# Two attention blocks on one core: moving Q for the second one in two half runs per group, and transposing P in bf16

## The chip, the core and the metric

The kernel runs on one core of a Trainium2 chip. The core has a matrix engine (TensorE, in the profile PE, with its weight loads shown apart as PEld), a vector engine (VectorE, DVE), an activation engine (ScalarE, ACT), GpSimd (POOL) and SyncE (SP). Each engine works through its own queue in order; they meet only through semaphores. Matmuls read SBUF and write PSUM, which has eight banks of 2 KB per partition; DVE and ACT read PSUM and write SBUF. SP issues the transfers from HBM, which run on 16 DMA engines. The metric is the time of one execution on the device, in microseconds (us); lower is better.

## The reference

Two independent blocks of cached attention; their outputs are joined on the last axis.

```python
# both: B, Sq, D = 16, 32, 1024;  32 query heads, Dh = 128;  Sk = 1024;  bf16
# A: 4 key/value heads, each used by 8 query heads;  B: 32 key/value heads
q = (x @ wq).reshape(B, Sq, 32, Dh).transpose(0, 2, 1, 3)
scores = einsum("bhqd,bhkd->bhqk", q, k) * Dh ** -0.5
p = softmax(scores, axis=-1)
o = einsum("bhqk,bhkd->bhqd", p, v)
block = o.transpose(0, 2, 1, 3).reshape(B, Sq, 32 * Dh) @ wo
out = concatenate([block_A, block_B], axis=-1)
```

Block A's K and V caches are 16.8 MB each, block B's 134.2 MB each; with the weights nearly 340 MB go through the core once.

## The kernel before

**Quads.** The work of each attention is cut into 128 quads. A quad is 128 rows of scores (four times 32 query tokens) against 1,024 keys. For the first attention (A, `pi == 0`) a quad is one batch entry and four of the eight query heads that share one K/V head; for the second (B, `pi == 1`) it is two batch entries and two heads, so four K/V pairs. Four B quads form a group: 128 tokens (four batch entries) and four heads. One B step takes one B quad, usually one A quad, and a share of projections.

**Stages of a quad**, in `st_scores` to `st_oev`: scores in PSUM (two banks, `ps_s`); the row maximum on DVE (line 837); the exponential on ACT, which writes P in bf16 to SBUF and sums its rows (line 850); the transpose of P on PE (line 862) into one of the four general banks `ps_g`; its eviction to `PT_sb` by ACT or DVE (line 526); the product with V on PE (line 884 for A, 892 for B); normalisation (lines 908 and 909), transpose of the output (line 914) and its eviction. P is transposed as f32: two neighbouring bf16 values are taken as one f32 element, so 1,024 columns are 512 elements and four 128x128 transposes suffice, and every piece reads its 128 columns four f32 elements (16 bytes) apart. After it each transposed element holds a pair, and `ptc_of` takes every second bf16 value as the weights of the PV matmul. So that a pair belongs to neighbouring chunks in A too, A's exponential reads its scores with a jump of 128 elements (line 845).

**B's K** is transposed in 32x32 blocks by DVE, two words at a time (line 785), and A's K by PE in eight 128x128 bf16 transposes (line 776), one eviction each.

**B's Q.** `qprojB` projects the queries of one group and head block (line 616) and evicts them to `Qtok`, which has a place for each of two head blocks and four groups. `qprepB_tr` transposes one group's Q on DVE into `QBt` (line 625). `qprepB_sh` moves it across partitions: for each of the group's four batch entries `a`, four 32x32 matmuls with an identity (line 638) copy row group `a` of `QBt` to all four row groups of one PSUM bank, 256 columns wide, and an eviction of 128x256 writes `QR`, the scores' weights. In step t of a group only `a = t % 4` of the next group is moved (line 1066).

**Order of the work.** The program adds operations to a list with their dependencies, and `list_schedule` simulates the engines with the durations in `DUR` and orders every engine's queue by it. Operations marked `any` go to ACT or DVE, whichever the simulation finds better. General banks, P, PT and other buffers are given out during that simulation (`slot_time`, `acquire`); banks of kind `pj` (projections and Q's move) have two of the four in reserve. The order in the queues is fixed from then on, and `finalize` adds semaphore waits. Between two operations of PE no wait is added (`_needs_wait`). All transfers are issued from SP's queue: B's V (line 763) waits for the PV that frees one of three buffers, B's K (line 750) for the DVE transpose that frees one of four.

Of the kernel before, what the change touches and what calls it, by code (L numbers as in the profile page):

```python
# [15 lines left out]
SCHED = True  # L16
NVB_SLOTS = 3
NKB_SLOTS = 2
LAZY_PER_STEP = 100
# [6 lines left out]
PRIO_BONUS = {}  # L26
PE_MODE = {"scoresB": 2, "Qshuf": 2, "PVB": 1}
MODE_SWITCH = 0.05
# [6 lines left out]
DUR = {  # L35
    "scoresB": (0.216, 0.20), "scoresA": (0.216, 0.20), "PT_trA": (0.49, 0.22), "PT_trB": (0.49, 0.22), "PVA": (0.45, 0.22), "PVB": (0.112, 0.22),
    "OT_tr": (0.056, 0.22), "KTA_tr": (0.45, 0.22), "Qshuf": (0.107, 0.20), "qprojA": (0.432, 0.20), "qprojB": (0.432, 0.20),
    "oprojA": (0.432, 0.20), "oprojB": (0.432, 0.20), "xT_tr": (0.45, 0.22),
    "exp": (1.10, 0.12), "PT_ev@act": (0.466, 0.13), "norm@act": (0.25, 0.13), "OT_ev@act": (0.11, 0.13), "KTA_ev@act": (0.466, 0.13),
    "qA_ev@act": (0.47, 0.13), "qB_ev@act": (0.478, 0.13), "QR_ev@act": (0.252, 0.13), "acc0@act": (0.47, 0.13), "acc0@dve": (0.58, 0.12), "xT_ev@act": (0.90, 0.13),  # L40
    "o_fin@act": (0.47, 0.13),
    "KBt_tr": (1.126, 0.11), "max": (1.12, 0.11), "recip": (0.06, 0.11), "norm@dve": (0.23, 0.13), "PT_ev@dve": (0.58, 0.12),
    "OT_ev@dve": (0.08, 0.12), "KTA_ev@dve": (0.58, 0.12), "QBt_tr": (0.345, 0.10), "acc+": (0.58, 0.12), "accF": (0.59, 0.12),
    "qA_ev@dve": (0.58, 0.12), "qB_ev@dve": (0.58, 0.12), "xT_ev@dve": (0.60, 0.12), "o_fin@dve": (0.58, 0.12), "QR_ev@dve": (0.30, 0.12),
    "c0": (0.2, 0.1), "c1": (0.3, 0.1),
# [60 lines left out]
class Prog:  # L106
# [116 lines left out]
    def list_schedule(self, lat=0.05, look=LOOK):  # L223
# [43 lines left out]
        def slot_time(i):  # L267

            t = 0.0
            for v in acq[i]:  # L270
# [40 lines left out]
        while True:  # L311
# [119 lines left out]
def build(nc, pa, pb, out):  # L431
# [34 lines left out]
    with stack:  # L466
# [6 lines left out]
        ident = sb("ident", [P, P], BF)  # L473
        zeros = sb("zeros", [P, P], BF)
        id32 = sb("id32", [P, P], F32)
        z32 = sb("z32", [P, P], F32)
# [34 lines left out]
        pr.add("pool", lambda g: g.memset(zeros[:], 0.0), writes=["zeros"], name="c0")  # L511
        pr.add("pool", lambda g: g.affine_select(ident[:], zeros[:], [[1, P]], ALU.not_equal, 1.0, base=0, channel_multiplier=-1),
               reads=["zeros"], writes=["ident"], name="c1")
        pr.add("pool", lambda g: g.memset(z32[:], 0.0), writes=["z32"], name="c0")
        pr.add("pool", lambda g: g.affine_select(id32[:], z32[:], [[1, P]], ALU.not_equal, 1.0, base=0, channel_multiplier=-1),
               reads=["z32"], writes=["id32"], name="c1")

# [89 lines left out]
        def qprojB(m_, G):  # L607
            lazy_flush(("wq", 1, m_))

            JS = 2 if DJ % 2 == 0 else 1  # L610
            v = Virt("bank", "pj")
            for j0 in range(0, DJ, JS):
                def e_qp(e, j0=j0):
                    last = None
                    for j in range(j0, j0 + JS):
                        last = e.matmul(bank(v)[:, 0:CW], xT_sb[:, 1, j, G * P:(G + 1) * P], wq_sb[:, 1, j, :], start=(j == 0), stop=(j == DJ - 1))  # L616
                    return last
                pcs = sorted(set(j * WQP // DJ for j in range(j0, j0 + JS)))
                pr.add("pe", e_qp, reads=[("wq", 1, k_) for k_ in pcs] + [("xT", 1, G)], writes=[v], claims=[("Qtok", m_ % 2, G)], name="qprojB", dur=0.225 * JS,
                       rtag=dict((("wq", 1, k_), m_) for k_ in pcs))  # L620
            evac(Qtok[:, m_ % 2, G, :], lambda: bank(v)[:, 0:CW], reads=[], writes=[v, ("Qtok", m_ % 2, G)], name="qB_ev",
                 wtag={("Qtok", m_ % 2, G): m_}, mul=scale)

        def qprepB_tr(m_, G):
            pr.add("dve", lambda e: e.transpose(QBt[:, :].bitcast(F32), Qtok[:, m_ % 2, G, :].bitcast(F32)),
                   reads=[("Qtok", m_ % 2, G)], writes=["QBt"], name="QBt_tr", rtag={("Qtok", m_ % 2, G): m_}, wtag={"QBt": (m_, G)})

        def qprepB_sh(m_, G, a_list):
            gp = (m_ * NG + G) % 2
            for a in a_list:  # L630
                v = Virt("bank", "pj")

                def e_sh(e, a=a, v=v):
                    last = None
                    for rg in range(4):
                        e_ = rg // 2
                        rhs = QBt[32 * a:32 * a + 32, :].rearrange("p (hp e x) -> p e hp x", hp=2, e=2)[:, e_, :, :]
                        last = e.matmul(bank(v)[32 * rg:32 * rg + 32, 0:2 * Dh].rearrange("p (hp x) -> p hp x", hp=2),
                                        ident[32 * a:32 * a + 32, 32 * a:32 * a + 32], rhs, start=True, stop=True,
                                        tile_position=(32 * a, 32 * rg))  # L640
                    return last
                pr.add("pe", e_sh, reads=["QBt", "ident"], writes=[v], claims=[("QR", gp, a)], name="Qshuf", rtag={"QBt": (m_, G)})
                evac(QR[:, gp, a, :, :], lambda v=v: bank(v)[:, 0:2 * Dh].rearrange("p (hp x) -> p hp x", hp=2), reads=[],
                     writes=[v, ("QR", gp, a)], name="QR_ev", wtag={("QR", gp, a): (m_, G)})

# [194 lines left out]
        def st_exp(q):  # L840
            vS, vP, vst = q.vS, q.vP, q.vst

            def emit(e):
                if q.pi == 0:
                    src = ps_s[:, vS.idx, :, :].rearrange("p u n -> p (u n)").rearrange("p (c k) -> p k c", c=NCH)
                    dst = P_sb[:, vP.idx, :].rearrange("p (k c) -> p k c", c=NCH)
                else:
                    src = ps_s[:, vS.idx, :, :].rearrange("p g (s j) -> p g j s", s=16)
                    dst = P_sb[:, vP.idx, :].rearrange("p (g j s) -> p g j s", g=2, s=16)
                return e.activation(dst, src, ACTF.Exp, bias=stat[:, vst.idx, 0:1], scale=1.0, accum_out=stat[:, vst.idx, 1:2])  # L850
            pr.add("act", emit, writes=vS.res + [vP, vst], name="exp")

        NPK = NCH // 2

        def st_ptr(q):
            vP, vPT, vb = q.vP, q.vPT, q.vbt

            def e_pt(e):
                last = None
                p32 = P_sb[:, vP.idx, :].bitcast(F32)  # L860
                for m in range(NPK):
                    last = e.transpose(bank(vb)[:, m * P:(m + 1) * P], p32[:, m:Sk // 2:NPK], id32[:])  # L862
                return last
            pr.add("pe", e_pt, reads=[vP, "id32", vPT], writes=[vb], name="PT_trA" if q.pi == 0 else "PT_trB")

# [145 lines left out]
        qprepB_tr(0, 0)  # L1011
        qprepB_sh(0, 0, [0, 1, 2, 3])
        for hh in range(MS):
# [37 lines left out]
        for t in range(NIT):  # L1051
# [73 lines left out]
```

## Time and profile before

| what | value |
|---|---|
| median of three runs | 903.89 us (901.42, 905.68, 903.89) |
| span of the profiled execution, first to last instruction | 902.6 us |
| mean granted TensorE clock | 0.985 |
| moved by DMA | 341.67 MB, mean 379 GB/s |
| transposes of P (line 862) on PE | 177.0 us busy, 1,024 pieces |
| exponentials (line 850) on ACT | 285.8 us busy, 256 |
| Q's move for B (line 638) on PE | 41.0 us busy, 512 matmuls |

The profiled execution's time is known as its span; the median of the runs shown is 1.3 us longer. "Busy" is the share of the span in which an engine had an instruction under way; on PE a matmul's time includes the pipeline, which the next one overlaps, so PE's cost is better read from the distance between starts. A group's line gives the line of the kernel, the engine, the operation, output and input tiles, the shape, the number, busy time, mean ns of one, and the idle time of the engine just before these instructions with what ended it.

### The profile page before, as it was taken

How to read it: one execution, taken by the hardware profiler on the slowest of the kernel's cores; microseconds unless marked ns; L12 is line 12 of the kernel's file. 1: busy time of each engine (PE TensorE's matmuls, PEld its weight loads, DVE VectorE, ACT ScalarE, POOL GpSimd, SP SyncE). 2: the span in 40 equal slices, each digit the busy share in tenths (PEclk: the TensorE clock that was granted, in tenths of full speed). 3: DMA queues.
4: the chain of work that ended last, by engine and by line, in shares of the span. 5: the costliest groups of instructions: out<-in, count | busy, mean ns of one | idle time of the engine just before them, and what ended most of it. 6: DMA issues, size and time to landing. Idle time of an engine off the chain costs nothing.

```text
span 902.6 us, 29455 instructions
## 1 busy us (share of the span) xinstructions
PE 836.3 (93%) x12864; PEld 481.8 (53%) x12864; DVE 745.3 (83%) x1057; ACT 610.8 (68%) x1384; POOL 1.1 (0%) x8
## 2 busy tenths in 40 slices
PE   6999999999899999999999998999998988999886
PEld 4365555555555555555545455555555554555453
DVE  0578897888887999689887899878979788798885
ACT  3477886677666776676776466776867666586763
POOL 0000000000000000000000000000000000000000
PEclk9999999999999999999999999999999999999999
DMA  9999999999999999999999999999999999999994
GB/s 325 383 389 393 386 385 392 390 393 383 392 387 389 393 380 388 380 386 376 387 385 391 394 369 389 388 393 370 388 387 391 392 391 367 344 393 393 393 377 170
DMA packets 153984, 341.67 MB, mean 379 GB/s; under 512 B 12544, under 2 KB 28928, under 8 KB 153856
## 3 DMA queue, kind: packets, MB, share of 16 engines
q1 hardware_dynamic: 153856, 339.79, 100.6%
q8 instruction: 102, 1.67, 0.8%
q14 instruction: 26, 0.21, 0.1%
HBM read 337.64 MB, written 2.10 MB: 376 GB/s over the span
## 4 chain that ended last, share of the span: by engine, by line
PE 48%; DMA 23%; DVE 19%; ACT 8%; SPq 1%; issue 1%; ACTq 0%; DVEq 0%
DMA KB_sb<-in_B_k_cache_dram 21%; PE ps_s L827 10%; PE ps_g L862 9%; DVE stat L837 8%; DVE KBt_sb L785 8%; PE ps_g L680 6%; ACT P_sb L850 5%; PE ps_g L892 4%; PE ps_g L598 4%; PE ps_g L884 4%; PE ps_g L616 3%; PE ps_s L806 3%; PE ps_g L776 2%; ACT PT_sb L526 1%; PE ps_g L914 1%
## 5 line engine op out<-in xcount | busy, mean ns | idle before, releaser
L785 DVE STREAM_TRANSPOSE KBt_sb<-KB_sb 128x1024 f32<-128x1024 f32 x256 | 311.8, 1231 | 42.5 <-DMA KB_sb<-in_B_k_cache_dram 40.4
L837 DVE TENSOR_REDUCE stat<-ps_s 128x1 f32<-128x1024 f32 x256 | 304.7, 1209 | 50.7 <-PE ps_s L827 34.3
L850 ACT ACTIVATE P_sb<-ps_s,stat 128x1024 bf16<-128x1024 f32 x256 | 285.8, 1119 | 51.5 <-DVE stat L837 50.0
L862 PE MATMUL ps_g<-id,P_sb 128*128 128x128 f32 x1024 | 177.0, 300 | 13.0 <-ACT P_sb L850 4.7
L862 PEld LDWEIGHTS ps_g<-id,P_sb 128*128 128x128 f32 x1024 | 150.5, 207 | 54.9 <-issue 11.1
L827 PE MATMUL ps_s<-KBt_sb,QR 32*32 32x512 bf16 x4096 | 157.2, 399 | 19.5 <-ACT P_sb L850 10.9
L526 ACT COPY PT_sb<-ps_g 128x512 f32<-128x512 f32 x234 | 134.9, 591 | 59.5 <-PE ps_g L862 58.3
L908 ACT ACTIVATE O_sb<-ps_g,stat 128x128 bf16<-128x128 f32 x199 | 71.4, 370 | 63.0 <-PE ps_g L892 32.4
L806 PE MATMUL ps_s<-KTA_sb,QT_sb 128*128 128x512 bf16 x256 | 91.5, 388 | 6.0 <-ACT P_sb L850 5.6
L827 PEld LDWEIGHTS ps_s<-KBt_sb,QR 32*32 32x32 bf16 x4096 | 49.3, 90 | 81.1 <-ACT P_sb L850 17.8
L892 PE MATMUL ps_g<-VB_sb,PT_sb 128*32 128x128 bf16 x4096 | 91.1, 224 | 1.4 <-ACT PT_sb L526 0.9
L892 PEld LDWEIGHTS ps_g<-VB_sb,PT_sb 128*32 128x32 bf16 x4096 | 60.2, 97 | 48.7 <-issue 29.2
L884 PE MATMUL ps_g<-VA_sb,PT_sb 128*128 128x128 bf16 x1024 | 78.8, 220 | 1.8 <-ACT PT_sb L526 0.7
L884 PEld LDWEIGHTS ps_g<-VA_sb,PT_sb 128*128 128x128 bf16 x1024 | 61.6, 98 | 28.2 <-issue 8.5
L616 PE MATMUL ps_g<-wq_sb,xT_sb 128*128 128x512 bf16 x256 | 71.4, 386 | 2.9 <-DMA wq_sb<-in_B_wq_dram 2.8
L680 PE MATMUL ps_g<-woB_sb,OTB_sb 128*128 128x512 bf16 x256 | 68.7, 381 | 4.4 <-ACT OTB_sb L526 1.8
L598 PE MATMUL ps_g<-xT_sb,wq_sb 128*128 128x512 bf16 x256 | 72.0, 385 | 0.3
L680 PE MATMUL ps_g<-woA_sb,OTA_sb 128*128 128x512 bf16 x256 | 63.0, 380 | 1.3 <-DVE OTA_sb L526 1.0
L914 PE MATMUL ps_g<-ident,O_sb 128*128 128x128 bf16 x256 | 51.8, 224 | 3.0 <-ACT O_sb L908 2.0
L850 ACT ACTIVATION_READ_ACCUMULATOR P_sb<-ps_s,stat 128x1 f32 x256 | 51.8, 202 | 0.0
L526 ACT COPY OTA_sb<-ps_g 128x64 f32<-128x64 f32 x114 | 24.7, 216 | 36.7 <-PE ps_g L914 36.1
L691 DVE TENSOR_TENSOR acc<-acc,ps_g 128x512 f32<-128x512 f32 x64 | 41.2, 675 | 8.1 <-PE ps_g L680 7.6
(41 smaller groups left out, 537.5 us busy)
## 6 DMA issues: line engine op xcount, KB each, us to landing
VB_sb<-in_B_v_cache_dram SPq DMA_DIRECT2D x256, 512.0 KB, 8.1
KB_sb<-in_B_k_cache_dram SPq DMA_DIRECT2D x256, 512.0 KB, 9.2
KA_sb<-in_A_k_cache_dram SPq DMA_DIRECT2D x64, 256.0 KB, 7.7
VA_sb<-in_A_v_cache_dram SPq DMA_DIRECT2D x64, 256.0 KB, 8.1
wq_sb<-in_B_wq_dram SPq DMA_DIRECT2D x32, 256.0 KB, 8.6
wq_sb<-in_A_wq_dram SPq DMA_DIRECT2D x32, 256.0 KB, 8.8
woB_sb<-in_B_wo_dram SPq DMA_DIRECT2D x32, 256.0 KB, 9.2
woA_sb<-in_A_wo_dram SPq DMA_DIRECT2D x32, 256.0 KB, 9.1
```

The costliest lines, as they stand in the source:

```text
L526: return e.copy(dst, src) if hasattr(e, "activation") else e.tensor_copy(dst, src)
L598: last = e.matmul(bank(v)[:, 0:tn], wq_sb[:, 0, j, hc * Dh:(hc + 1) * Dh], xT_sb[:, 0, j, t0:t0 + tn], start=(j == 0), stop=(j == DJ - 1))
L616: last = e.matmul(bank(v)[:, 0:CW], xT_sb[:, 1, j, G * P:(G + 1) * P], wq_sb[:, 1, j, :], start=(j == 0), stop=(j == DJ - 1))
L680: last = e.matmul(bank(v)[:, 0:OUTW], OT[:, gp, hh, :], wo_[:, hh, oh * OUTW:(oh + 1) * OUTW], start=(hh == 0), stop=(hh == nh - 1))
L785: pr.add("dve", lambda e: e.transpose(KBt_sb[:, sl, t_, :].bitcast(F32), KB_sb[:, rs, :].bitcast(F32)), reads=[("KB", rs)], writes=[("KBt" ...
L806: pr.add("pe", lambda e, u=u: e.matmul(ps_s[:, vS.idx, u, :], qt[:, q.b, q.hh0:q.hh0 + 4, :].rearrange("p a q -> p (a q)"), KTA_sb[:, sl, ...
L827: last = e.matmul(ps_s[32 * cg:32 * cg + 32, vS.idx, g2, :].rearrange("p (s j) -> p s j", s=16), lhsT, rhs, start=(fp == 0), stop=(fp == 3 ...
L837: pr.add("dve", lambda e: e.tensor_reduce(stat[:, vst.idx, 0:1], ps_s[:, vS.idx, :, :], AXIS.XY, ALU.max, negate=True), writes=vS.res + [v ...
L850: return e.activation(dst, src, ACTF.Exp, bias=stat[:, vst.idx, 0:1], scale=1.0, accum_out=stat[:, vst.idx, 1:2])
L862: last = e.transpose(bank(vb)[:, m * P:(m + 1) * P], p32[:, m:Sk // 2:NPK], id32[:])
L884: last = e.matmul(bank(vb)[:, 0:Dh], ptc_of(vPT, c, 0, P), VA_sb[:, kvs, c, :], start=(c == 0), stop=(c == NCH - 1))
L892: last = e.matmul(bank(vb)[32 * a:32 * a + 32, 0:Dh], ptc_of(vPT, c, 32 * a, 32 * a + 32), VB_sb[:, kvs, a // 2, a % 2, c, :], start=(c == ...
```

## The change

1. P is transposed as bf16: eight 128x128 pieces into the same bank, `P_sb[:, c*128:(c+1)*128]` for A and `P_sb[:, c:1024:8]` for B. The eviction stays one 128x512 f32 copy. A's exponential reads its scores in order; PV takes its weights without gaps. The f32 identity goes, and the bf16 one is made in place.
2. All of a group's Q is moved in one step (`t % 4 == 0`), in two half runs: `Qshuf` for entries 0 and 2, `Qshuf2` for 1 and 3, eight matmuls each. Entries 0 and 1 fill one bank, 2 and 3 the other, and each bank is evicted by one 128x512 operation. Both half runs write both banks, so `Qshuf2` waits for `Qshuf`: the first wait of PE for itself. The planner's bank test now counts two banks taken by one operation.
3. `Qtok` is a ring of five group slots instead of eight.
4. Planned durations: transposes of P 0.49 -> 0.45, Q's moves 0.107 -> 0.15, their evictions 0.252 -> 0.478 (ACT) and 0.30 -> 0.58 (DVE).

```diff
+        if (d.name, op.name) == ("Qshuf", "Qshuf2"):
+            return True
...
-                if len(idle) <= keep:
+                if len(idle) <= keep + nth:
                     return None
-                t = max(t, sorted(idle)[0])
+                t = max(t, sorted(idle)[nth])
...
-                same_pe = (op.dma_key is None and beng == uo.eng and uo.eng == "pe")
+                same_pe = (op.dma_key is None and beng == uo.eng and uo.eng == "pe" and uo.name != "Qshuf2")
...
-        Qtok = sb("Qtok", [P, 2, NG, CW], BF)
+        Qtok = sb("Qtok", [P, NQT, CW], BF)
...
+            vv = [Virt("bank", "pj"), Virt("bank", "pj")]
+
+            def e_sh(e, aa):
+                last = None
+                for a in aa:
+                    out_ = bank(vv[a // 2])[:, (a % 2) * 2 * Dh:(a % 2 + 1) * 2 * Dh].rearrange("p (hp x) -> p hp x", hp=2)
+                    src_ = QBt[32 * a:32 * a + 32, :].rearrange("p (hp e x) -> p e hp x", hp=2, e=2)
                     for rg in range(4):
...
+                        last = e.matmul(out_[32 * rg:32 * rg + 32], ident[32 * a:32 * a + 32, 32 * a:32 * a + 32], src_[:, rg // 2, :, :],
+                                        start=True, stop=True, tile_position=(32 * a, 32 * rg))
+                return last
+            for name, aa in (("Qshuf", (0, 2)), ("Qshuf2", (1, 3))):
+                pr.add("pe", lambda e, aa=aa: e_sh(e, aa), reads=["QBt", "ident"], writes=vv, claims=[("QR", gp, a) for a in aa], name=name,
+                       rtag={"QBt": (m_, G)})
+            for b in range(2):
+                evac(QR[:, gp, 2 * b:2 * b + 2, :, :].rearrange("p a hp x -> p (a hp x)"), lambda b=b: bank(vv[b]), reads=[],
+                     writes=[vv[b], ("QR", gp, 2 * b), ("QR", gp, 2 * b + 1)], name="QR_ev",
...
-                    src = ps_s[:, vS.idx, :, :].rearrange("p u n -> p (u n)").rearrange("p (c k) -> p k c", c=NCH)
-                    dst = P_sb[:, vP.idx, :].rearrange("p (k c) -> p k c", c=NCH)
+                    src = ps_s[:, vS.idx, :, :].rearrange("p u n -> p (u n)")
+                    dst = P_sb[:, vP.idx, :]
...
-                p32 = P_sb[:, vP.idx, :].bitcast(F32)
-                for m in range(NPK):
-                    last = e.transpose(bank(vb)[:, m * P:(m + 1) * P], p32[:, m:Sk // 2:NPK], id32[:])
+                for c in range(NCH):
+                    pc = P_sb[:, vP.idx, c * P:(c + 1) * P] if q.pi == 0 else P_sb[:, vP.idx, c:Sk:NCH]
+                    last = e.transpose(bankb(vb)[:, c * P:(c + 1) * P], pc, ident[:])
...
-            return PT_sb[:, vPT.idx, :, :].rearrange("p c q -> p (c q)").rearrange("p (m r two) -> p m r two", m=NPK, two=2)[:, c // 2, lo:hi, c % 2]
+            return PT_sb[:, vPT.idx, c, lo:hi]
...
                 if t % 4 == 0:
                     qprepB_tr(qn.m, qn.G)
-                qprepB_sh(qn.m, qn.G, [t % 4])
+                    qprepB_sh(qn.m, qn.G)
```

More of the change, by code (lines that the diff above doesn't have):

```diff
@@ L17 @@
 NVB_SLOTS = 3
+NQT = 5
 NKB_SLOTS = 2
@@ L26 @@
 PRIO_BONUS = {}
-PE_MODE = {"scoresB": 2, "Qshuf": 2, "PVB": 1}
+PE_MODE = {"scoresB": 2, "Qshuf": 2, "Qshuf2": 2, "PVB": 1}
 MODE_SWITCH = 0.05
@@ L43 @@
     "OT_ev@dve": (0.08, 0.12), "KTA_ev@dve": (0.58, 0.12), "QBt_tr": (0.345, 0.10), "acc+": (0.58, 0.12), "accF": (0.59, 0.12),
-    "qA_ev@dve": (0.58, 0.12), "qB_ev@dve": (0.58, 0.12), "xT_ev@dve": (0.60, 0.12), "o_fin@dve": (0.58, 0.12), "QR_ev@dve": (0.30, 0.12),
+    "qA_ev@dve": (0.58, 0.12), "qB_ev@dve": (0.58, 0.12), "xT_ev@dve": (0.60, 0.12), "o_fin@dve": (0.58, 0.12), "QR_ev@dve": (0.58, 0.12),
     "c0": (0.2, 0.1), "c1": (0.3, 0.1),
@@ L269, in slot_time @@
             t = 0.0
-            for v in acq[i]:
+            for k_, v in enumerate(acq[i]):
+                nth = sum(1 for w in acq[i][:k_] if w.cls == v.cls)
                 idle = [slot_free[v.cls][x] for x in range(SLOTS[v.cls]) if held[v.cls][x] is None]
                 keep = sum(k for kind, k in BANK_RESERVE.items() if kind != v.kind and not any(h is not None and h.kind == kind for h in held["bank"])) if v.cls == "bank" else 0
-                if len(idle) <= keep:
+                if len(idle) <= keep + nth:
                     return None
-                t = max(t, sorted(idle)[0])
+                t = max(t, sorted(idle)[nth])
             return t
@@ L509, in build @@
             print("sbuf bytes remaining per partition:", nc.sbuf_bytes_remaining() if callable(nc.sbuf_bytes_remaining) else nc.sbuf_bytes_remaining)
[L511 to L516, printed above, removed]
+        pr.add("pool", lambda g: g.memset(ident[:], 0.0), writes=["ident"], name="c0")
+        pr.add("pool", lambda g: g.affine_select(ident[:], ident[:], [[1, P]], ALU.not_equal, 1.0, base=0, channel_multiplier=-1),
+               writes=["ident"], name="c1")
         def evac(dst_ap, src_ap, reads, writes, name, eng=None, wtag=None, rtag=None, mul=None):
@@ L618, in qprojB @@
                 pcs = sorted(set(j * WQP // DJ for j in range(j0, j0 + JS)))
-                pr.add("pe", e_qp, reads=[("wq", 1, k_) for k_ in pcs] + [("xT", 1, G)], writes=[v], claims=[("Qtok", m_ % 2, G)], name="qprojB", dur=0.225 * JS,
+                pr.add("pe", e_qp, reads=[("wq", 1, k_) for k_ in pcs] + [("xT", 1, G)], writes=[v], claims=[("Qtok", (m_ * NG + G) % NQT)], name="qprojB", dur=0.225 * JS,
                        rtag=dict((("wq", 1, k_), m_) for k_ in pcs))
-            evac(Qtok[:, m_ % 2, G, :], lambda: bank(v)[:, 0:CW], reads=[], writes=[v, ("Qtok", m_ % 2, G)], name="qB_ev",
-                 wtag={("Qtok", m_ % 2, G): m_}, mul=scale)
+            qs = (m_ * NG + G) % NQT
@@ L624, in qprepB_tr @@
+            evac(Qtok[:, qs, :], lambda: bank(v)[:, 0:CW], reads=[], writes=[v, ("Qtok", qs)], name="qB_ev",
+                 wtag={("Qtok", qs): (m_, G)}, mul=scale)
         def qprepB_tr(m_, G):
-            pr.add("dve", lambda e: e.transpose(QBt[:, :].bitcast(F32), Qtok[:, m_ % 2, G, :].bitcast(F32)),
-                   reads=[("Qtok", m_ % 2, G)], writes=["QBt"], name="QBt_tr", rtag={("Qtok", m_ % 2, G): m_}, wtag={"QBt": (m_, G)})
-        def qprepB_sh(m_, G, a_list):
+            qs = (m_ * NG + G) % NQT
@@ L629, in qprepB_sh @@
+            pr.add("dve", lambda e: e.transpose(QBt[:, :].bitcast(F32), Qtok[:, qs, :].bitcast(F32)),
+                   reads=[("Qtok", qs)], writes=["QBt"], name="QBt_tr", rtag={("Qtok", qs): (m_, G)}, wtag={"QBt": (m_, G)})
+        def qprepB_sh(m_, G):
             gp = (m_ * NG + G) % 2
[L630 to L634, printed above, removed]
-                    for rg in range(4):
[L636 to L644, printed above, removed]
@@ new lines, in qprepB_sh @@
+            for name, aa in (("Qshuf", (0, 2)), ("Qshuf2", (1, 3))):
[4 more added lines that the diff above has]
+                     writes=[vv[b], ("QR", gp, 2 * b), ("QR", gp, 2 * b + 1)], name="QR_ev",
+                     wtag={("QR", gp, 2 * b): (m_, G), ("QR", gp, 2 * b + 1): (m_, G)})
@@ L851, in st_exp @@
             pr.add("act", emit, writes=vS.res + [vP, vst], name="exp")
-        NPK = NCH // 2
         def st_ptr(q):
@@ L859, in e_pt @@
                 last = None
-                p32 = P_sb[:, vP.idx, :].bitcast(F32)
-                for m in range(NPK):
-                    last = e.transpose(bank(vb)[:, m * P:(m + 1) * P], p32[:, m:Sk // 2:NPK], id32[:])
+                for c in range(NCH):
+                    pc = P_sb[:, vP.idx, c * P:(c + 1) * P] if q.pi == 0 else P_sb[:, vP.idx, c:Sk:NCH]
+                    last = e.transpose(bankb(vb)[:, c * P:(c + 1) * P], pc, ident[:])
                 return last
-            pr.add("pe", e_pt, reads=[vP, "id32", vPT], writes=[vb], name="PT_trA" if q.pi == 0 else "PT_trB")
+            pr.add("pe", e_pt, reads=[vP, "ident", vPT], writes=[vb], name="PT_trA" if q.pi == 0 else "PT_trB")
         def st_pev(q, eng=None):
@@ L1011, in build @@
         qprepB_tr(0, 0)
-        qprepB_sh(0, 0, [0, 1, 2, 3])
+        qprepB_sh(0, 0)
         for hh in range(MS):
```

9 lines of the change are left out of this document (3 added, 6 removed).

## The prediction

> **What bounds the kernel now.** First the profile's page: engine totals, the bandwidth row, and the chain that ended last.
>
> ```profile
> PE 836.3 (93%) x12864; PEld 481.8 (53%) x12864; DVE 745.3 (83%) x1057; ACT 610.8 (68%) x1384; POOL 1.1 (0%) x8
> GB/s 325 383 389 393 386 385 392 390 393 383 392 387 389 393 380 388 380 386 376 387 385 391 394 369 389 388 393 370 388 387 391 392 391 367 344 393 393 393 377 170
> q1 hardware_dynamic: 153856, 339.79, 100.6%
> PE 48%; DMA 23%; DVE 19%; ACT 8%; SPq 1%; issue 1%; ACTq 0%; DVEq 0%
> ```
>
> The bandwidth row has a ceiling of 393 GB/s that many slices reach and none but one (394) passes. A slice is 902.6 / 40 = 22.56 us. Summing (393 - rate) / 393 x 22.56 us gives 3.9 us lost in the first slice, 12.8 us in the last and only 16.5 us in all 38 between. So the transfers are nearly the bound: if compute never held them up again in the middle, the span would be 902.6 - 16.5 = 886 us. No saving on an engine can bring more than that, short of the two ends. PE's 93% says that there is little room the other way.
>
> Next the groups by shape, for the operations that the change touches and for their nearest neighbours.
>
> ```profile
> L850 ACT ACTIVATE P_sb<-ps_s,stat 128x1024 bf16<-128x1024 f32 x256 | 285.8, 1119 | 51.5 <-DVE stat L837 50.0
> L862 PE MATMUL ps_g<-id,P_sb 128*128 128x128 f32 x1024 | 177.0, 300 | 13.0 <-ACT P_sb L850 4.7 <-ACT OTA_sb L526 3.2 <-ACT OTB_sb L526 1.8
> L776 PE MATMUL ps_g<-ident,KA_sb 128*128 128x128 bf16 x512 | 39.2, 219 | 1.1 <-ACT OTA_sb L526 0.7 <-DVE acc L691 0.4
> L638 PE MATMUL ps_g<-QBt,ident 32*32 32x256 bf16 x512 | 41.0, 277 | 2.0 <-DVE acc L691 1.0 <-ACT acc L526 0.7
> L526 ACT CAST QR<-ps_g 128x256 bf16<-128x256 f32 x101 | 37.8, 381 | 14.7 <-PE ps_g L638 11.8 <-PE ps_s L827 1.9
> L526 DVE CAST QR<-ps_g 128x256 bf16<-128x256 f32 x27 | 11.0, 411 | 0.9 <-PE ps_g L638 0.8
> L526 ACT COPY KTA_sb<-ps_g 128x512 f32<-128x512 f32 x46 | 27.5, 597 | 5.2 <-PE ps_g L776 5.1
> L526 ACT COPY xT_sb<-ps_g 128x1024 bf16<-128x1024 bf16 x6 | 5.8, 1015 | 4.7 <-PE ps_g L546 4.7
> ```
>
> A matmul's duration includes pipeline time that the next one overlaps, so its cost is read from starts on PE's timeline:
>
> ```profile
> 304.57 0.28 PE L638 MATMUL ps_g<-QBt,ident 32*32 32x256 bf16 x2
> 305.16 0.29 PE L638 MATMUL ps_g<-QBt,ident 32*32 32x256 bf16 x4
> 305.38 0.75 PE L862 MATMUL ps_g<-id,P_sb 128*128 128x128 f32 x4
> 305.97 0.59 PE L616 MATMUL ps_g<-wq_sb,xT_sb 128*128 128x512 bf16 x2
> 306.40 0.61 PE L776 MATMUL ps_g<-ident,KA_sb 128*128 128x128 bf16 x8
> 306.85 0.59 PE L616 MATMUL ps_g<-wq_sb,xT_sb 128*128 128x512 bf16 x2
> ```
>
> Four f32 transposes hold PE 305.97 - 305.38 = 0.59 us; eight bf16 ones (of KA_sb, stored without gaps) 306.85 - 306.40 = 0.45 us, although there are twice as many. Over the whole timeline the medians are 0.58 and 0.54 us, since the run of eight is often followed by a 32-row operation, and then its last piece takes 0.149 us in place of 0.056: changing between tilings costs about 0.09 us.
>
> Last, who holds the transfers up, on SP's queue:
>
> ```profile
> SPq L763 <- PE ps_g L892: 136.7, 69, 7.4
> SPq L750 <- DVE KBt_sb L785: 115.2, 77, 5.2
> ```
>
> SP waits for a PV to free a V buffer, or for the DVE to free a K buffer. Issues take 8 to 9 us to land at 393 GB/s, so most of this waiting passes while earlier transfers still flow.
>
> **The change, part by part.**
>
> P's transposes. 1,024 f32 pieces go, 2,048 bf16 pieces come. For the first attention the pieces are now gapless, like KA_sb's: 0.58 -> 0.54 us per quad. For the second they step by 8 bf16, 16 bytes, and no bf16 weight load in the trace does that. Bounds: the row of KA_sb (0.056 us a piece), and the f32 pieces, which step by the same 16 bytes: (0.75 - 0.29) / 3 = 0.15 us at most, about 0.12 in the longer runs. I take the KA_sb value, because element type and shape agree with it, and PT_sb's reads at line 884, with a step of 4 bytes, also run at 0.056. Then PE's demand falls by 256 x 0.04 = 10 us. Line 862 holds 8.7% of the chain, 78.5 us, so 78.5 x 0.04 / 0.58 = 5.4 us leave the path.
>
> [...]
>
> Exponential of the first attention. Its PSUM read is now without gaps (it jumped 128 f32 per element). Both forms take 1.12 us now, and both jump. Bounds: no change, and the gapless 1,024-element copy at 1.015 us, -0.10 us. That row is a copy from bf16, so I take the middle, -0.05: 128 x 0.05 = 6 us of ACT. L850 is 4.9% of the chain, 44 us, half of it the first attention's: 22 x 0.05 / 1.12 = 1 us of path.
>
> Q's move. 128 runs of four matmuls become 64 of eight; all 512 matmuls stay. Entering the 32-row tiling 64 times fewer saves up to 64 x 0.09 = 5.8 us on PE; at PE's 48% of the chain, 2.8 us of path. Evictions: 37.8 + 11.0 = 48.8 us on ACT and DVE become 64 x 0.597 = 38.2 us, -10 us. L526 for QR is not among the chain's listed lines, so I count nothing; that cover is lost only where scores wait for QR.
>
> The added wait. The second half run waits for the first to finish. Lower bound 0 (other PE work is placed between; the planner now makes it ready 0.40 us after the first starts); upper bound a whole matmul, 0.28 us, and about 0.1 us of signalling. I take 0.15: 32 x 0.15 = 4.8 us of PE, 2.3 of path. Behind it stand all later PE operations, so ACT's PT and O evictions and SP's V loads inherit what is not filled.
>
> Two banks at once. Of four general banks a group holds two until both are evicted; before, one four times. The bank time is less (two evictions of 0.6 for four of 0.38 with their own waits), the peak is higher. From 0 to 0.4 us of delay per group to the PT and PV that find no bank; I take 0 and keep the rest for a rival.
>
> Nothing: the Qtok ring. Group g's slot was last read by group g-5's DVE transpose, planned at second-attention step 4(g-6), which is at least five steps (some 35 us) before the projection that refills it. Also nothing: two POOL operations fewer at 0.7 to 2.0 us, since PE's first use waits for x until 3.52 us; contiguous weights for PV, at 0.056 already. No DMA is moved by name; the planner reorders SP's issues by new durations, of either sign, perhaps 3 us.
>
> Sum on the path: -5.4 - 1 - 2.8 + 2.3 = -6.9 us, well inside the 16.5. The profiled execution's span 902.6 becomes 895.7; the median of the runs shown, 903.9, is 1.3 above that span, so **897 us**.
>
> **Rivals.**
>
> *Hidden (no change, 904 us).* The dips come from DVE, not PE: K transposes and maxima are 312 + 305 us of DVE and alternate on the chain. For: 115 us of SP's waits end on L785. Against: the larger 137 end on PV. Then the 6.9 us only lengthen waits.
>
> *Strided pieces slow (928 us, slower).* If each 16-byte step costs a piece of the second attention 0.12 us, as the f32 pieces with this step do, a run becomes 8 x 0.12 + 0.09 = 1.05 us: +0.47 x 128 = 60 us, less 5 for the first attention and about 6 elsewhere, +49 us on PE. PE has 902.6 - 836.3 = 66 us idle; half absorbed gives 902.6 + 24.5 + 1.3 = 928, all absorbed 904, none 953. It decides once a piece exceeds 0.58 / 8 = 0.073 us. For: the only row with this step is slow. Against: that row is f32 as well, and cannot separate the two.
>
> [...]
>
> *Bank squeeze (911 us, slower).* Two banks taken together stall PT and PV by 0.4 us in each of 32 groups, 13 us, against savings of half the 6.9. For: evictions of 0.6 us hold both; PE already waits for bank-freeing ACT lines. Against: a bank is busy under half the time by the sums of the rows.
>
> **How the numbers follow.** Forecast 0.44 (own range 891 to 902: dips recovered twice as much, or almost not), hidden 0.18, strided 0.22, squeeze 0.16. Half a per cent, 4.5 us, is what a measurement tells (the runs span 901.4 to 905.7). Faster: 0.33 of the forecast's and 0.02 of the hidden = 0.35. Same: 0.11 + 0.14 + 0.02 of the squeeze = 0.27. Slower: 0.22 + 0.14 + 0.02 = 0.38. Range 890 to 926: it leaves out the upper half of the strided case (0.11) and 0.03 below.
>
> **What would show it.** L862's successor: bf16 starts 0.056 us apart in the first attention (right); in the second 0.056 (forecast) or 0.1 and above (strided rival), with PE busy up by some 50 us. L850: a first-attention form below the second's 1.12. QR evictions: 64 of about 0.6. PE idle ended by PE itself at the second half run: under 5 us. Middle bandwidth losses down from 16.5 to about 10 us. PT waiting for bank-freeing evictions, up by 10 us, would speak for the squeeze; unchanged dips with more idle PE for the hidden case.

## The result

The changed kernel takes 898.5 us (897.8 to 900.9, four runs) against 904.75 us for the kernel before on the same chip: a ratio of 0.994, 95% interval 0.9915 to 0.9966, faster by 0.6%. These two times are medians, 6.3 us apart; the means, 898.9 and 904.1 us, whose quotient is the ratio, are 5.2 us apart. The forecast was 897 us. Its direction and its size came out; the runs below show that its reason did not.

The profiled execution's span fell from 902.6 to 896.0 us. The granted clock was 0.985 in the first and 0.998 in the second of these executions; a second profile of the changed kernel, at 0.990, has a span of 897.8 us. So a part of the 6.6 us between the two spans goes with the clock (more on this under "Where the time went"). From the profile's page of the changed kernel, the engine totals, the bandwidth in 40 slices and the chain by engine:

```profile
PE 790.8 (88%) x13712; PEld 461.5 (52%) x13888; DVE 746.5 (83%) x1040; ACT 608.4 (68%) x1337; POOL 0.7 (0%) x6
GB/s 320 384 386 396 394 388 390 381 378 393 391 388 389 391 391 383 384 393 390 389 386 388 393 385 378 390 388 391 388 385 384 389 396 395 388 389 393 381 386 189
PE 35%; DMA 34%; DVE 20%; ACT 7%; issue 2%; SPq 2%; DVEq 0%; ACTq 0%
```

By the same sum as before, against 393 GB/s (slices above 393 count as no loss), the 38 middle slices now lose 10.9 us (16.5 before), the first 4.2 (3.9) and the last 11.6 (12.8). The dip of 367 and 344 in two neighbouring slices is gone. PE's share of the chain fell from 48% to 35%, that of the transfers rose from 23% to 34%. PE's total is too low here, because 176 matmul records are missing (13,712 beside 13,888 weight loads); the second profile, with all of them, has 812.9 us, 23 less than before.

The groups by shape that answer to those shown of before:

```profile
L853 ACT ACTIVATE P_sb<-ps_s,stat 128x1024 bf16<-128x1024 f32 x256 | 285.5, 1117 | 63.9 <-DVE stat L840 60.5 <-PE ps_g L863 0.7
L863 PE MATMUL ps_g<-ident,P_sb 128*128 128x128 bf16 x2048 | 163.5, 225 | 13.1 <-ACT P_sb L853 3.0 <-ACT PT_sb L524 1.9 <-ACT OTB_sb L524 1.5
L638 PE MATMUL ps_g<-QBt,ident 32*32 32x256 bf16 x512 | 20.8, 281 | 3.5 <-DVE QBt L625 1.2 <-ACT OTA_sb L524 0.6
L524 ACT CAST QR<-ps_g 128x512 bf16<-128x512 f32 x50 | 27.6, 590 | 14.2 <-PE ps_g L638 14.2
L524 DVE CAST QR<-ps_g 128x512 bf16<-128x512 f32 x14 | 9.3, 672 | 1.4 <-PE ps_g L638 1.4
```

Line 853 is the exponential (850 before), 863 the transposes of P (862 before). The exponential still takes 1.12 us, so reading A's scores in order brought nothing. Q's evictions fell from 48.8 to 27.6 + 9.3 = 36.9 us. Q's 512 matmuls, still as many, fell from 41.0 to 20.8 us busy.

PE's timeline shows the two forms of a transpose run, and Q's move:

```profile
310.35 0.65 PE L863 MATMUL ps_g<-ident,P_sb 128*128 128x128 bf16 x8
310.84 1.03 PE L683 MATMUL ps_g<-woB_sb,OTB_sb 128*128 128x512 bf16 x4
...
317.98 0.70 PE L638 MATMUL ps_g<-QBt,ident 32*32 32x256 bf16 x16
318.61 0.23 PE L915 MATMUL ps_g<-ident,O_sb 128*128 128x128 bf16 x1
...
324.71 0.61 PE L863 MATMUL ps_g<-ident,P_sb 128*128 128x128 bf16 x8
325.25 0.63 PE L893 MATMUL ps_g<-VB_sb,PT_sb 128*32 128x128 bf16 x32
```

The run of 0.65 us occupies PE for 0.49 us and has a start every 0.061 us or so; the one of 0.61 us has one every 0.056. Over the whole timeline the first attention's runs are of the second kind and the second attention's lie at 0.061 to 0.070: the pieces with the 16-byte step are dearer by about a tenth to a quarter, not by a factor of two. Both half runs of Q's move, sixteen matmuls, take 318.61 - 317.98 = 0.63 us with their wait between; before, a run of four took 0.22 us at the median from its first start to the next operation, so four such runs 0.88 us. The wait is this row of line 638:

```profile
its engine sat idle before it (us, times) until:
  PE ps_g L638: 4.6, 16
```

### The profile page after: what moved, and what is told of

Its sections match the earlier page's. It is cut to its first block, busy times and chain, and to the rows that moved or that the text cites. A ratio compares the mean times of both kernels' runs of the same rounds, so it can differ in the third digit from the quotient of the medians.

```text
span 896.0 us, 31269 instructions
## 1 busy us (share of the span) xinstructions
PE 790.8 (88%) x13712; PEld 461.5 (52%) x13888; DVE 746.5 (83%) x1040; ACT 608.4 (68%) x1337; POOL 0.7 (0%) x6
## 4 chain that ended last, share of the span: by engine, by line
PE 35%; DMA 34%; DVE 20%; ACT 7%; issue 2%; SPq 2%; DVEq 0%; ACTq 0%
DMA KB_sb<-in_B_k_cache_dram 32%; DVE KBt_sb L788 10%; PE ps_s L830 8%; DVE stat L840 7%; PE ps_g L863 6%; PE ps_g L683 5%; ACT P_sb L853 5%; PE ps_g L596 3%; PE ps_g L893 3%; PE ps_g L614 2%; PE ps_g L885 2%; PE ps_s L809 2%; PE ps_g L915 1%; PE ps_g L779 1%; ACT PT_sb L524 1%
## 5 line engine op out<-in xcount | busy, mean ns | idle before, releaser
L853 ACT ACTIVATE P_sb<-ps_s,stat 128x1024 bf16<-128x1024 f32 x256 | 285.5, 1117 | 63.9 <-DVE stat L840 60.5
L830 PE MATMUL ps_s<-KBt_sb,QR 32*32 32x512 bf16 x4096 | 154.2, 394 | 34.0 <-ACT P_sb L853 20.1
L524 ACT COPY PT_sb<-ps_g 128x512 f32<-128x512 f32 x233 | 134.9, 589 | 65.3 <-PE ps_g L863 63.9
L863 PE MATMUL ps_g<-ident,P_sb 128*128 128x128 bf16 x2048 | 163.5, 225 | 13.1 <-ACT P_sb L853 3.0
L863 PEld LDWEIGHTS ps_g<-ident,P_sb 128*128 128x128 bf16 x2048 | 139.9, 123 | 63.6 <-ACT P_sb L853 11.6
L909 ACT ACTIVATE O_sb<-ps_g,stat 128x128 bf16<-128x128 f32 x198 | 71.0, 370 | 43.0 <-PE ps_g L893 21.6
L893 PE MATMUL ps_g<-VB_sb,PT_sb 128*32 128x128 bf16 x4096 | 87.4, 221 | 6.1 <-ACT PT_sb L524 1.6
L614 PE MATMUL ps_g<-wq_sb,xT_sb 128*128 128x512 bf16 x223 | 64.7, 389 | 6.1 <-issue 2.0
L683 PE MATMUL ps_g<-woB_sb,OTB_sb 128*128 128x512 bf16 x234 | 62.5, 380 | 7.6 <-ACT OTB_sb L524 3.2
L809 PE MATMUL ps_s<-KTA_sb,QT_sb 128*128 128x512 bf16 x174 | 61.7, 382 | 6.6 <-ACT P_sb L853 1.4
L596 PE MATMUL ps_g<-xT_sb,wq_sb 128*128 128x512 bf16 x233 | 64.6, 380 | 2.4 <-issue 1.3
L683 PE MATMUL ps_g<-woA_sb,OTA_sb 128*128 128x512 bf16 x240 | 59.4, 380 | 2.9 <-issue 1.7
```

The lines of the kernel that those rows point to most:

```text
L524: return e.copy(dst, src) if hasattr(e, "activation") else e.tensor_copy(dst, src)
L596: last = e.matmul(bank(v)[:, 0:tn], wq_sb[:, 0, j, hc * Dh:(hc + 1) * Dh], xT_sb[:, 0, j, t0:t0 + tn], start=(j == 0), stop=(j == DJ - 1))
L683: last = e.matmul(bank(v)[:, 0:OUTW], OT[:, gp, hh, :], wo_[:, hh, oh * OUTW:(oh + 1) * OUTW], start=(hh == 0), stop=(hh == nh - 1))
L809: pr.add("pe", lambda e, u=u: e.matmul(ps_s[:, vS.idx, u, :], qt[:, q.b, q.hh0:q.hh0 + 4, :].rearrange("p a q -> p (a q)"), KTA_sb[:, sl, ...
L830: last = e.matmul(ps_s[32 * cg:32 * cg + 32, vS.idx, g2, :].rearrange("p (s j) -> p s j", s=16), lhsT, rhs, start=(fp == 0), stop=(fp == 3 ...
L863: last = e.transpose(bankb(vb)[:, c * P:(c + 1) * P], pc, ident[:])
```

## The experiments

The theory at the start was that PE's relief on the path made the gain, and that Q's move, whose PE time halved, was the larger part. Rival 1 was the prediction's own sum, in which the transposes lead. Rival 2 was the order: the change also alters planned durations, and every queue is reordered by them.

### One part at a time

```diff
# e1_pt_only: kernel before with
-    "PT_trA": (0.49, 0.22), "PT_trB": (0.49, 0.22)
+    "PT_trA": (0.45, 0.22), "PT_trB": (0.45, 0.22)
...
-                for m in range(NPK):
-                    last = e.transpose(bank(vb)[:, m * P:(m + 1) * P], p32[:, m:Sk // 2:NPK], id32[:])
+                for c in range(NCH):
+                    pc = P_sb[:, vP.idx, c * P:(c + 1) * P] if q.pi == 0 else P_sb[:, vP.idx, c:Sk:NCH]
+                    last = e.transpose(bankb(vb)[:, c * P:(c + 1) * P], pc, ident[:])
...
```

> The kernel before with the transposes of P alone changed (bf16 pieces, A's exponential in order, planned duration 0.45); Q's move as before. Theory (relief of PE on the path, Q's move the larger part): PE busy falls by about 15 us, a quarter of the gain, ratio 0.998 to 1.000. Rival 1 (the transposes are the cause, as the prediction's sum had it): ratio 0.993 to 0.995. Rival 2 (the new order of the queues is the cause): any ratio, and the run with the durations alone shows the same.

Measured: 901.56 us, ratio 0.9973 (0.9958 to 0.9989), between the theory's range and rival 1's.

```diff
# e2_q_only: changed kernel with
-    "PT_trA": (0.45, 0.22), "PT_trB": (0.45, 0.22)
+    "PT_trA": (0.49, 0.22), "PT_trB": (0.49, 0.22)
...
-                    last = e.transpose(bankb(vb)[:, c * P:(c + 1) * P], pc, ident[:])
+                    last = e.transpose(bank(vb)[:, m * P:(m + 1) * P], p32[:, m:Sk // 2:NPK], id32[:])
...
```

> The changed kernel with P transposed as f32 again, so Q's move alone is changed. Theory: eight matmuls of a half run take PE's time of four, so line 638 falls from 41 to 21 us busy and most of the gain is here, ratio 0.994 to 0.997. Rival 1 (the transposes are the cause): ratio 0.998 to 1.001. Rival 2 (order): not told by this run alone.

Measured: 901.06 us, ratio 0.9971 (0.9955 to 0.9987), at the edge of the theory's range; the matmuls of Q's move take 21.6 us busy.

```diff
# e3_durations_only: kernel before with
-    "PT_trA": (0.49, 0.22), "PT_trB": (0.49, 0.22)
+    "PT_trA": (0.45, 0.22), "PT_trB": (0.45, 0.22)
```

> The kernel before with the planned duration of P's transposes set from 0.49 to 0.45 and nothing else: the same instructions in another order. Theory: within 0.3% of the kernel before (0.997 to 1.003), so that a gain of 0.6% is more than reordering. Rival 2 (the gain is the order's luck): 0.995 or lower, or a loss of as much.

Measured: 900.32 us, ratio 0.9962 (0.9945 to 0.9979). This is the surprise: the same instructions as before, told to the planner as 0.04 us shorter, bring 0.38%, two thirds of the whole gain. The expectation of at most 0.3% was missed.

> The changed kernel once more, beside the others on one chip. All theories: ratio 0.992 to 0.997.

Measured: 899.2 us, ratio 0.9944 (0.9927 to 0.996).

The run with the transposes and the new duration is no faster than the one with the new duration alone, and their queues hold the same operations in the same order. That is against rival 1, and leaves the theory and rival 2.

### The pieces at a fixed order, and other orders

The planner's order depends on planned durations and dependencies, not on what an instruction really costs. So two kernels that differ only in f32 or bf16 pieces can be given the same queues, and the same instructions different ones.

```diff
# e5_bf16_old_order: kernel before with bf16 pieces, duration left at 0.49
-                    last = e.transpose(bank(vb)[:, m * P:(m + 1) * P], p32[:, m:Sk // 2:NPK], id32[:])
+                    last = e.transpose(bankb(vb)[:, c * P:(c + 1) * P], pc, ident[:])
...
```

> The kernel before with the transposes of P in bf16 (and A's exponential in order), but with the old planned duration 0.49, so that every queue holds the same operations in the same order as before. Theory (the transposes in themselves bring little, since the run with the durations alone already gained 0.38% and the one with both 0.27%): ratio 0.998 to 1.002. Rival 1 (the prediction's largest term, 5.4 us of path from the transposes): 0.993 to 0.996.

Measured: ratio 0.9998 (0.9983 to 1.0013). At fixed order the transposes bring nothing.

```diff
# e6_after_049: changed kernel with
-    "PT_trA": (0.45, 0.22), "PT_trB": (0.45, 0.22)
+    "PT_trA": (0.49, 0.22), "PT_trB": (0.49, 0.22)
```

> The changed kernel with the planned duration of P's transposes put back to 0.49: its queues are those of the run with Q's move alone, so the two differ only in f32 against bf16 pieces. Theory: the same ratio as that run, 0.997, within 0.2%. Rival 1 (transposes): 0.3 to 0.6% faster than that run, 0.991 to 0.994. Rival 2 (order): a ratio clearly apart from the changed kernel's 0.994.

Measured: ratio 0.9997 (0.9981 to 1.0014). All of the change's instructions, in the order for 0.49, bring nothing that can be measured. That is far from the 0.9944 of the same instructions in the order for 0.45, and the strongest single result for rival 2. It is also no better than its twin with f32 pieces (0.9971). The expectation was that the two are equal within 0.2%; why they differ by 0.26% is open.

```diff
# e7_before_051 and e8_before_047: kernel before with
-    "PT_trA": (0.49, 0.22), "PT_trB": (0.49, 0.22)
+    "PT_trA": (0.51, 0.22), "PT_trB": (0.51, 0.22)   # e8: 0.47
```

> The kernel before with the planned duration of P's transposes at 0.51: the same instructions in a third order. If the order alone moves the time by some 0.4%, this one lies anywhere from 0.995 to 1.005; if the kernel before is an ordinary order, it stays within 0.2% of 1.

Measured: ratio 0.9994 (0.998 to 1.0008).

> The kernel before with the planned duration at 0.47, a fourth order of the same instructions. The same expectation: with the two others it gives the spread that reordering alone makes (0.995 to 1.005 if order matters, 0.998 to 1.002 if it does not).

Measured: ratio 1.0 (0.9982 to 1.0018).

So the kernel before is an ordinary order of its instructions; of its four orders only the one for 0.45 is faster.

### The missing cell, and another order of the changed kernel

```diff
# e9_f32_q_045: changed kernel with f32 pieces, duration left at 0.45
-                    last = e.transpose(bankb(vb)[:, c * P:(c + 1) * P], pc, ident[:])
+                    last = e.transpose(bank(vb)[:, m * P:(m + 1) * P], p32[:, m:Sk // 2:NPK], id32[:])
...
```

> Q's move changed, P transposed as f32, planned duration 0.45: the queues of the changed kernel with the old pieces in them. It is the cell that was still missing of pieces, Q's move and planned duration. Theory (the pieces bring nothing; Q's move and the order that 0.45 gives bring the gain together): the changed kernel's ratio, 0.993 to 0.996. If the pieces matter after all in this order: 0.997 or above.

Measured: 898.82 us, ratio 0.9949 (0.9928 to 0.997): the changed kernel's time with the old pieces.

```diff
# e12_after_047: changed kernel with
-    "PT_trA": (0.45, 0.22), "PT_trB": (0.45, 0.22)
+    "PT_trA": (0.47, 0.22), "PT_trB": (0.47, 0.22)
```

> The changed kernel with the planned duration at 0.47: a third order of its instructions (0.45 gave 0.994, 0.49 gave 1.000). If 0.45 is a lucky order and Q's move brings about 0.2% by itself: 0.997 to 0.999. If the changed kernel is faster in most orders: 0.995 or lower. If only the order matters: 0.999 to 1.001.

Measured: ratio 0.9953 (0.9935 to 0.997): between the first two expectations, nearer to "faster in most orders".

All ratios together:

| planned duration | pieces | Q's move as before | Q's move in two half runs |
|---|---|---|---|
| 0.45 | f32 | 0.9962 | 0.9949 |
| 0.45 | bf16 | 0.9973 | 0.9944 |
| 0.47 | f32 / bf16 | 1.0 (f32) | 0.9953 (bf16) |
| 0.49 | f32 | 1 (the kernel before) | 0.9971 |
| 0.49 | bf16 | 0.9998 | 0.9997 |
| 0.51 | f32 | 0.9994 | |

Reading down, bf16 against f32 at the same queues: +0.0011, -0.0005, -0.0002, +0.0026, on average +0.0008, nothing or a shade slower. Reading across, averaged over the pieces: Q's half runs bring 0.2% at 0.45, 0.5% at 0.47 (there with different pieces) and 0.15% at 0.49. Between 0.49 and 0.45 either column moves by 0.3 to 0.4% on average. Each difference carries 0.2 to 0.3% of uncertainty, and the rows were measured on three chips, each beside the kernel before.

### Is PE's time worth anything?

```diff
# e11_half_projections: changed kernel with
-                    for j in range(j0, j0 + JS):
+                    for j in range(j0, j0 + 1):
...
```

> The changed kernel with every second matmul of the Q projections left out in both attentions (256 of 512, so Q is only half summed); queues otherwise in the same order, all transfers as before. PE has 256 x 0.216 = 55 us less to do. Theory (transfers are the bound, 10.9 us lost in the middle): at most these come back, 886 to 897 us. Rival (PE is the bound): about half of 55 us comes back, 870 us.

Measured: 898.76 us, ratio 0.9941 (0.9921 to 0.9962), the changed kernel's ratio (0.994 and 0.9944) within the noise, and outside both expectations. From its page:

```profile
PE 748.3 (83%) x13459; PEld 441.3 (49%) x13632; DVE 747.2 (83%) x1040; ACT 608.1 (68%) x1337; POOL 0.7 (0%) x6
GB/s 320 383 386 395 394 388 392 385 369 390 390 387 391 389 393 388 379 391 388 391 385 390 394 387 377 390 389 388 391 386 385 390 395 392 390 389 394 376 384 169
```

By the distance of starts PE has 55 us less to do (its busy time falls by 790.8 - 748.3 = 42.5 us, with about as many records missing in both), and neither the time nor the bandwidth moves (11.4 us lost in the middle). Once the changed kernel's order is given, further relief of PE is worth nothing. Against the theory that PE's time on the path made the gain this is an argument and no proof: in the kernel before, PE was relieved at a fixed order only by e5's transposes, which brought nothing; Q's projections were not halved there.

```diff
# e10_second_twice: changed kernel with
-                for c in range(NCH):
+                for c in list(range(NCH)) * (2 if q.pi == 1 else 1):
```

> The changed kernel with every transpose of the second attention's P made twice (the same pieces again, so nothing else changes and the queues keep their order): 1,024 more pieces with the 16-byte step, some 0.06 to 0.07 us each, 60 to 70 us more for PE. The prediction's price for the strided rival (half absorbed by idle PE, half on the span) makes that 930 us, ratio 1.03. If PE has slack to hide it, 905 us or less; if PE is the bound, 960.

Measured: 932.5 us, ratio 1.0319 (1.0295 to 1.0343). From its page (bandwidth, and the chain by engine, 70% PE) and its groups:

```profile
GB/s 327 383 387 379 360 383 351 370 364 393 381 365 368 375 381 380 366 388 346 379 371 356 389 355 378 368 387 366 380 383 365 366 387 383 371 375 390 362 379 144
PE 70%; DVE 14%; ACT 11%; issue 3%; DMA 2%; SPq 0%; ACTq 0%; DVEq 0%
L863 PE MATMUL ps_g<-ident,P_sb 128*128 128x128 bf16 x3072 | 227.4, 226 | 10.0 <-ACT P_sb L853 2.0 <-ACT OTB_sb L524 1.3 <-ACT PT_sb L524 1.3
```

Line 863 rises by 227.4 - 163.5 = 63.9 us, the time by 34 us, just over half, and the bandwidth row now loses 42.9 us in the middle. So in these two runs PE's time is worth nothing downwards and a half upwards: the changed kernel stands at the edge between the two bounds.

### Where the time went

From the trace of each run, the start of the last of B's 256 K transposes on DVE, what remains from there to the end, and the granted clock of that execution:

| kernel | Q's move | planned | last K transpose, us | from there to the end, us | granted clock |
|---|---|---|---|---|---|
| before | as before | 0.49 | 887.8 | 14.7 | 0.985 |
| e5 | as before | 0.49 | 885.3 | 15.7 | 0.989 |
| e8 | as before | 0.47 | 884.3 | 16.2 | 0.991 |
| e7 | as before | 0.51 | 883.1 | 17.4 | 0.991 |
| e3 | as before | 0.45 | 884.5 | 15.2 | 0.983 |
| e1 | as before | 0.45 | 886.0 | 15.0 | 0.985 |
| e2 | half runs | 0.49 | 882.3 | 17.4 | 0.991 |
| e6 | half runs | 0.49 | 882.4 | 17.4 | 0.994 |
| e12 | half runs | 0.47 | 881.9 | 14.2 | 0.994 |
| e9 | half runs | 0.45 | 881.3 | 14.7 | 0.993 |
| changed kernel | half runs | 0.45 | 881.9 | 14.2 | 0.998 |
| the same again | half runs | 0.45 | 882.8 | 15.0 | 0.990 |

These are single executions; the two of the changed kernel differ by 0.9 us in the one column and 0.8 in the other. Three things are apart here.

First, all six profiles with half runs (five kernels, one of them twice) reach the last K transpose before all six others, on average at 882.1 against 885.2 us: 3 us. Two things on record make less of this. Their granted clock was higher, on average 0.993 against 0.987. Over the 178 executions recorded with the experiments, taken kernel by kernel, one with a clock lower by 0.01 took about 3 us longer; by that, an estimate, 2 of the 3 us go with the clock. And the lead opens late: at the 232nd of the 256 transposes both groups stand at 809.2 us on average, whereas a gain of every move of Q would have grown over the whole run.

The clock does not explain the ratios measured over many executions: its mean was 0.988 for e3, which is faster, and 0.991 for the kernel before beside it, and 0.989 for both with e12. The largest difference in favour of a faster kernel, 0.993 against 0.989 with e9, is worth about 1 us of its 5.

Second, the kernel before is late even among its own kind, by 887.8 - 885.2 = 2.6 us. Its bandwidth dipped to 367 and 344 in two neighbouring slices, 4.3 us by the sum. The bf16 pieces in the same order (e5) show the same dip, 378 and 336, 4.1 us:

```profile
GB/s 319 383 389 394 387 387 391 390 386 373 392 390 388 395 390 386 388 392 380 391 385 390 386 387 389 383 391 367 395 388 391 391 391 378 336 389 393 397 392 165
```

In the same two slices e3, in the order for 0.45, has 389 and 385, 0.7 us:

```profile
GB/s 326 382 390 394 390 385 389 379 386 393 391 387 390 394 395 384 388 391 376 392 383 389 394 380 396 381 393 372 393 390 392 390 396 389 385 392 387 396 349 142
```

The order for 0.45 with bf16 pieces (e1) has 385 and 372, 1.7 us, the one for 0.47 (e8) 375 and 364, 2.7 us, the one for 0.51 (e7) 388 and 394, 0.2 us. So the dip does not come from the pieces. Whether the order makes it, or the clock of these executions, is not shown: between 740 and 790 us the granted clock was 0.93 in the kernel before, 0.90 in e5, 0.93 in e1, 0.97 in e8 and e3 and 1.00 in e7; in the profiles with half runs, which have no dip, it was 1.00 but for one of 0.97. Nor is a missing dip a gain by itself, since e7 has none and its ratio is 0.9994.

Third, the end after the last K transpose is a matter of order too, 14.2 to 17.4 us. In the changed kernel's timeline of the last quads (DVE, ACT and the scores on PE):

```profile
879.57 1.25 DVE L788 STREAM_TRANSPOSE KBt_sb<-KB_sb 128x1024 f32<-128x1024 f32 x1 [0.27 <-PE ps_s L830]
880.74 1.19 DVE L840 TENSOR_REDUCE stat<-ps_s 128x1 f32<-128x1024 f32 x1
881.85 1.22 DVE L788 STREAM_TRANSPOSE KBt_sb<-KB_sb 128x1024 f32<-128x1024 f32 x1
881.96 1.11 ACT L853 ACTIVATE P_sb<-ps_s,stat 128x1024 bf16<-128x1024 f32 x1 [0.50 <-DVE stat L840]
883.31 1.13 PE L830 MATMUL ps_s<-KBt_sb,QR 32*32 32x512 bf16 x32 [2.10 <-ACT P_sb L853]
885.79 1.13 ACT L853 ACTIVATE P_sb<-ps_s,stat 128x1024 bf16<-128x1024 f32 x1
```

and with the same instructions in the order for 0.49 (e6):

```profile
881.22 2.37 DVE L788 STREAM_TRANSPOSE KBt_sb<-KB_sb 128x1024 f32<-128x1024 f32 x2
883.52 2.32 DVE L840 TENSOR_REDUCE stat<-ps_s 128x1 f32<-128x1024 f32 x2
884.74 1.11 ACT L853 ACTIVATE P_sb<-ps_s,stat 128x1024 bf16<-128x1024 f32 x1 [0.66 <-DVE stat L840]
886.00 1.87 PE L830 MATMUL ps_s<-KBt_sb,QR 32*32 32x512 bf16 x32 [2.17 <-ACT P_sb L853]
889.39 1.12 ACT L853 ACTIVATE P_sb<-ps_s,stat 128x1024 bf16<-128x1024 f32 x1
```

In the first, DVE takes a maximum between the last two K transposes, so ACT's exponential starts at 881.96, frees the score banks, and the last quad's scores start at 883.31. In the second, DVE makes both K transposes and then both maxima; the exponential starts at 884.74 and PE waits for it until 886.00, although the last K has been ready since 883.59. Everything behind it is later by about as much: the last exponential starts 3.6 us later. Of e6's disadvantage in its span, 3.7 us, 3.2 lie here, with the same instructions; e2, with f32 pieces in that order, has the same 17.4. The kernel before has a good end (14.7), so this part explains the spread among the orders and only about half a microsecond of the change itself.

What Q's move itself brings is open. The kernel with half of its projections left out reaches the last K transpose at 882.6 us, no earlier than the changed kernel; that shows only that less PE work brings no further lead there, not that the lead over the kernel before has nothing to do with PE's time. Fewer evictions on ACT and DVE (36.9 for 48.8 us), fewer and other bank holdings, or merely the orders that the planner finds with the new form may be behind it; the planner gives no common order to the two forms of the move. That the lead opens only in the last 24 transposes speaks for the orders. The planned durations of Q's own moves and evictions, which the change also alters, were not run alone in the kernel before.

## Why the prediction was right, and where its steps were not

- *Bound.* Right as far as it was tested, on the changed kernel: no PE saving recovers more than the middle's losses, and there is little room the other way. e11 (nothing for 55 us less) and e10 (34 us for 64 more) show both sides.
- *Transposes, -5.4 us of path.* Wrong. PE's cost of a run was sized about right (0.54 us, and somewhat more for B's), but it was turned into time by line 862's share of the chain. e5 and e9 measure that time as 0, within 0.2%. The chain is one path that ended last; that others stood beside it, those of the transfers above all, so that a share of it was no price, is the likely reason and was not shown apart.
- *Exponential, -1 us.* Wrong in its small way: 1.118 us for the form in order against 1.120 for the form with a jump. The row taken as the nearest, a copy from bf16, did not carry over.
- *Q's move, -2.8 us.* The size of PE's saving was missed, since eight matmuls of two row groups passed in 0.23 us, where four of one had taken 0.22: 20 us less busy, or by starts 128 x 0.22 - 64 x 0.23 = 13 us, not 5.8. The half runs go with 0.15 to 0.5% of the time, for a reason that is open.
- *The added wait, 4.8 us on PE.* The sum was right, its factors were not: PE stood idle 4.6 us at line 638 for itself, 16 times 0.29 us and not 32 times 0.15. Where a second half run followed at once, it started 0.371 us after the last start of the first (median of 16), a matmul of 0.278 us and 0.093 more, so the upper bound's terms were about right. What the wait cost in time was not measured apart.
- *Two banks at once, and the ring of five.* Right: no squeeze is seen; before P's transposes PE and its weight loads now wait 31 us for evictions, 28 before, where 10 more were to be the sign. The squeeze's price of 911 us does not follow from its own terms, which give 903.9 + 13 - 3.45 = 913 us. With a ring of eight slots the planner makes exactly the same queues.
- *The planner's new order, "of either sign, perhaps 3 us".* This is the step that failed. It was rightly sized but entered with zero; it is the largest term that was measured, 0.38% or 3.4 us in the kernel before, and 0.5% in the changed one between 0.49 and 0.45. In the single traces it goes with the missing dip and, among other orders, with the end.
- *The strided rival.* Its price was right (930 us expected of 64 us more, 932.5 measured); its condition was not met, with starts at 0.061 to 0.070 us below the 0.073 at which it would have decided. The 0.12 us a piece of the f32 row did not carry over to bf16. The bf16 loads with that step took 0.14 to 0.17 us (median 0.147), the f32 loads with it 0.20 to 0.23 (0.209), and bf16 loads without it 0.10 (0.098); of the 0.05 us by which the step lengthened the bf16 loads, 0.005 to 0.014 shows in the starts.
- *The hidden rival.* Its outcome held wherever PE's work alone was shortened (e5, e11); that the dips come from DVE, its mechanism, was not tested.

So the sum of -6.9 us met the measured -6.3 us (5.2 by the means) with wrong terms, and that is luck: 5.4 of it is 0, and the order, set to 0, is half of the whole or more.

## What to carry to other kernels

Where a planner lays out the queues, a change to a planned duration is a change of its own: run it alone, and run the new instructions in the old order, before a gain is put down to them. A share of the chain did not price the saving here (5.4 us expected, 0 measured within 0.2%): beside transfers that lost only 10.9 us of the middle slices against 393 GB/s, 55 us less work on the busiest engine was worth nothing, and 64 us more cost half of it. The last few steps, after the last load, are worth a look of their own: with the same instructions, one maximum placed after a K transpose instead of before it went with 3 us. And before two single traces are compared to a few microseconds, their granted clocks are: here 0.01 went with 3 us.

## What the runs showed of the hardware

- Eight 32x32 matmuls of 256 columns from row groups 0 and 2 into two banks took PE hardly longer than four from one row group: in the second profile of the changed kernel, eight that were followed at once by other work passed in 0.23 us at the median from the first start to the next operation, four did in the kernel before in 0.22.
- PE's wait for its own previous matmuls lengthened, in the changed kernel, the distance from the last of the eight starts to the next operation from 0.21 to 0.37 us.
- Weight loads of 128 bf16 columns with a step of 16 bytes took 0.14 to 0.17 us in the changed kernel, those without gaps 0.10; the matmuls behind them started every 0.061 to 0.070 us instead of 0.056.
- The exponential of A's 1,024 f32 scores from PSUM took 1.120 us with a jump of 128 elements (kernel before) and 1.118 in order (changed kernel), means of 128 each.
- Among executions of one kernel, those with a mean granted TensorE clock lower by 0.01 took about 3 us of 900 longer (178 executions; in their profiles the clock falls short in stretches, as to 0.66 from 745 to 750 us in the kernel before).
